# One schedule table of a fused RWKV-7 and squared-ReLU kernel exchanged for another

## Chip, cores and metric

The kernel runs on one core of one Trainium2 chip. The metric is the device time of one execution in microseconds (us). TensorE is called PE here, VectorE DVE, ScalarE ACT, GpSimd POOL, and the queue that issues most DMAs is SyncE's, SP.

## What is computed

For each of 4 batches and 8 heads a 40x40 state is carried over 768 steps, and the outputs go through a two-layer network with a squared ReLU:

```python
for t in range(S):                       # B=4, H=8, S=768, D=40
    y[:, :, t] = einsum('bhd,bhde->bhe', rt, state)
    Sa = einsum('bhde,bhe->bhd', state, at)
    state = state * wt[:, :, None, :] - einsum('bhd,bhe->bhde', Sa, bt) \
            + einsum('bhd,bhe->bhde', vt, kt)
x = y as (B*S, H*D)                      # 3072 x 320
h = x @ w_in                             # 320 -> 2048
out = maximum(h, 0)**2 @ w_out           # 2048 -> 320
```

## The kernel before

The 768 steps are cut into 6 chunks of 128. A chunk of one batch is a *piece* m (24 of them, m = 4 * chunk + batch); half a piece, four heads, is a *half* st (48). Four pieces of a chunk feed 8 *units* n of the network's first layer (48 units), and each piece has one output tile.

The life of a piece, by the names of the functions: six loads (`lW lK lB lA lV lR`, 160 KB each; R of pieces 0 to 15 comes for two chunks in one load of 320 KB); the decays (`b_ln` on ACT, `b_cs` on PE, `b_cx` on DVE, `b_xi` and `b_gp` on ACT); the products with the decays, rounded to bfloat16 (`b_pk` writes KBp, `b_pa`, `b_cv` and `b_cr` write their parts of RVAp, `b_gw` writes Gp); turned copies of them, by PE and a copy out of PSUM (`b_kt` and `b_kv` for KBT; `b_ta`/`b_at`, `b_vm`/`b_vv`, `b_rn`/`b_rv` for RV) or by a transposing DMA (`b_rt`, `b_aa`, `b_ka`, on SP's queue). Then for each half `st_a_mm` makes products `ca`, which are copied to CN with a triangular mask; `b_p`, `corr`, `b_c1`, `b_sn` solve for the piece's correction in the PSUM tile P; `b_x` sums its parts on POOL; `st_ex_mm` makes `ex`, copied to EX with the mask; `st_z`, `st_kb` make outputs and the next state in `uy`; `st_y`, `st_u` (DVE) move them to YN and UZ; `b_xt`, `b_xv` turn the outputs to XS. The network: `f_r`, `f_m` fill two PSUM tiles `hp`, `f_e` writes their ReLU to hs on ACT, `f_q` squares hs into Gt, `f_o` multiplies by WOUT, `f_v` copies `op_` to osb, `f_w` sends it out.

The order of all of it is written out by hand in one table, `ORDER`: 1937 tokens of the form `name.number`, with the PSUM bank behind `@` and the engine (D, A or P) behind `:` where there is a choice. Each engine takes its own tokens in that order and waits by semaphores; so do SP's loads.

```python
WORK = {"a": st_a_mm, "av0": bind(st_a_ev, 0), ..., "pk": b_pk, "pa": b_pa, ...}
def masked(by, out, in_):
    if by == "A":                        # plain copy on ACT, then a cut on POOL (cut_off)
        nc.scalar.activation(out=out, in_=in_[:], func=ACTF.Copy)
    else:                                # copy and mask in one, on DVE
        nc.vector.tensor_tensor(out=out, in0=in_[:], op=ALU.mult, in1=MEX...)
for tok in ORDER.split():
    act(tok)
```

So a mask on ACT costs ACT one instruction (line 346) and POOL one (line 353, AFFINE_SELECT); a mask on DVE (line 348) costs DVE one. Tokens `w` are matmuls without a use, which fill PE's waits at the start. The natural loads have four buffers a kind, hs two. The last two outputs (22 and 23) are copied and sent behind a branch, which a check of the numbers decides.

Of the kernel before, what the change touches and what calls it, by code (L numbers as in the profile page):

```python
# [18 lines left out]
def kernel(  # L19
# [23 lines left out]
    NB, NHH, T, D = r.shape  # L43
# [622 lines left out]
    def get_flag():  # L666
# [4 lines left out]
        lW.0 lK.0 f.0:D f.13:D f.1:P w.13@1 ln.0 w.2@u f.3:D lW.1 f.14:P f.17:P f.20:D lV.0 f.5:D  # L671
        lB.0 f.12:P i.0 f.19:D f.4:P w.15@x f.2:D ln.1 i.1 cv.0:A lK.1 w.3@e f.6:P w.1@u lA.0
        cs.0@e f.9:P cs.1@1 f.11:D xi.1 w.0@s lB.1 vm.0@u cx.0 xi.0 pk.0:D lA.1 w.8@s lV.1 f.8:P
        w.14@0 lR.0 gp.0 kt.0@f pa.0:D ta.0@f i.2 cx.1 vv.0:A f.18:D w.11@0 pk.1:P lW.2 w.9@u
        kv.0:D at.0:A a.0@xe f.16:D a.1@f0 f.10:D gp.1 kt.1@u pa.1:P av0.0:A av1.1:D w.6@1 ta.1@0
        kv.1:A w.4@s av1.0:D at.1:D a.2@fe av0.2:A aq0.0 w.16@1 lW.3 aq1.1 cv.1:A gw.0:D gc.0@0
        cr.0:P gl.0 ln.2 av0.1:D aq0.1 av1.2:D a.3@xu aq0.2 aq1.0 av0.3:A lK.2 aq0.3 w.7@1 cs.2@f
        p.0@1 gw.1:P rn.0@0 av1.3:D ln.3 aq1.2 cx.2 f.15:P m.0:A vm.1@x lR.1 aq1.3 rn.4@f k1.0
        lA.2 vv.1:A lB.2 p.1@s f.7:D cs.3@e lV.3 gp.2 c.0 lW.5 cr.1:A lK.3 m.1:D xi.2 rv.4:D xi.3
        pa.2:P k2.0 k1.1 c.1 s.0:A rv.0:A cx.3 pk.2:D gw.2:P k2.1 t.0@1 ta.2@f w.12@e s.1:A t.1@u  # L680
        x.1 tv.0:A tv.1:D at.2:A rn.5@0 e.1@xs rn.1@f ev1.1:D gp.3 rv.1:D rv.5:A lA.3 lB.3 kt.2@e
        e.3@0u cv.3:P ln.5 kv.2:D e.0@sf lW.4 a.4@fe ev0.1:A jk.1 eq1.1 ev0.0:D a.5@s1 pa.3:P
        eq0.1 cs.5@x av0.4:D av1.5:D lR.2 ev1.3:A ev0.3:A ta.3@1 xi.5 av1.4:D w.10@u pk.3:P aq0.4
        av0.5:A cx.5 kt.3@f aq1.5 z.1@0 e.2@es ev1.0:D ln.4 at.3:A kv.3:D eq1.3 kb.1 aq0.5 a.6@x1
        gl.1 wt.0 eq1.0 lV.2 lR.3 lA.4 ev0.2:A cs.4@u u.1 z.0@f av0.6:D lK.4 cv.2:P wt.2 eq0.0
        kb.0 av1.6:A y.1 x.0 z.3@e aq1.4 p.2@1 gp.5 cr.2:P en.1 lB.4 cx.4 eq0.3 m.2:D xi.4 u.0 y.0
        gp.4 a.7@xf k1.2 wt.6 vm.2@u aq1.6 lK.5 vm.3@0 c.2 av0.7:D pa.4:D aq0.6 wt.7 k2.2 cr.3:A
        eq0.2 av1.7:D lB.5 vv.2:D xt.0@x wd.0 rn.6@f lA.5 kb.3 s.2:A aq1.7 gw.3:P rn.2@1 gw.4:D
        ev1.2:A wd.1 ta.4@s lV.4 aq0.7 xv.0:A rn.7@u wt.3 wt.1 t.2@f p.3@x rv.6:D at.4:D rv.2:A
        m.3:D rv.7:A tv.2:A vv.3:D jk.2 wt.4 k1.3 rn.3@u e.4@ff lW.6 e.5@s0 y.3 eq1.2 c.3 pk.4:D  # L690
        k2.3 wt.5 ev0.4:A z.2@1 gl.2 s.3:D kt.4@f jk.0 kb.2 ev1.5:D u.3 kv.4:A eq0.4 u.2 x.2 t.3@e
        rv.3:A y.2 ev0.5:D gw.5:D xt.1@f ev1.4:D xv.1:A jk.3 a.8@ux a.9@ff tv.3:D eq1.4 fa.0 eq0.5
        e.6@e1 av0.8:A av1.9:A lK.6 pk.5:D fr.0@s0 wt.8 lV.5 ev0.6:D z.4@u ev1.6:D wt.9 kb.4 u.4
        z.6@f av0.9:A z.5@f lA.6 aq0.8 fb.0 pa.5:P eq1.6 eq1.5 ra.0 av1.8:A kb.5 aq0.9 y.4 gl.3
# [272 lines left out]
```

## Time and profile before

| | before |
|---|---|
| time, median of 3 runs | 258.82 us (258.47 to 259.81) |
| the profiled execution | 259.36 us, span 257.7 us |
| busy: PE, DVE, ACT, POOL | 243.3, 207.9, 207.8, 203.2 us |
| moved by DMA | 37.40 MB, 145 GB/s on average |

A busy PE is one with a matmul in flight; since matmuls overlap, that is no measure of how well it is fed, and idle time of PE is what is to be read. Lines such as L348 are lines of the kernel's file.

### The profile page before, as it was taken

The page shows a single profiled execution, that of the slowest core. Times are in us where ns is not written, and L with a number is a line of the kernel's source. Part 1 is how long each engine was busy: PE and PEld are TensorE (multiplying, and loading weights), DVE is VectorE, ACT ScalarE, POOL GpSimd, SP SyncE. Part 2 cuts the span into 40 slices and gives each one's busy share as a digit, 9 for nine tenths or more (in the row PEclk, how much of TensorE's full clock was granted, in tenths as well). Part 3 has the DMA queues.
Part 4 walks back from the last instruction along what each step waited for, and adds up shares of the span by engine and source line. Part 5 has one row for each costly group of instructions (what it writes and reads, how often), then busy time and mean ns, then how long its engine had stood idle before and what let it go on. Part 6 is the DMA issues. An engine that isn't in the chain of part 4 may idle for free.

```text
span 257.7 us, 9653 instructions
## 1 busy us (share of the span) xinstructions
PE 243.3 (94%) x3925; PEld 195.3 (76%) x3925; DVE 207.9 (81%) x435; ACT 207.8 (81%) x482; POOL 203.2 (79%) x235
## 2 busy tenths in 40 slices
PE   7986978999998999999999999999999999999992
PEld 3555666889886788787878888887888878888871
DVE  5597998799989899896999779989887799776220
ACT  3679898799987789887896799988796969799530
POOL 6469999839795499889789879888959777989770
PEclk9999997999999999999999999999999999999999
DMA  7999999999905997996999988988799985510011
GB/s 127 200 164 205 175 176 195 156 188 162 211 18 119 163 178 152 188 172 111 182 164 176 194 151 159 169 163 152 115 194 178 134 161 99 135 53 25 29 57 59
DMA packets 171924, 37.40 MB, mean 145 GB/s; under 512 B 167520, under 2 KB 170592, under 8 KB 171872
## 3 DMA queue, kind: packets, MB, share of 16 engines
q1 hardware_dynamic: 170528, 34.09, 76.1%
q0 software_dynamic: 1344, 2.62, 6.1%
q8 instruction: 32, 0.52, 0.9%
q14 instruction: 20, 0.16, 0.2%
HBM read 28.84 MB, written 3.93 MB: 127 GB/s over the span
## 4 chain that ended last, share of the span: by engine, by line
PE 64%; DVE 8%; DMA 8%; ACT 6%; SPq 5%; POOL 3%; issue 3%; POOLq 0%; DVEq 0%; ACTq 0%
PE hp L588 18%; SPq L95 4%; PE ex L456 4%; PE ca L333 3%; PE cs L191 3%; PE P L390 3%; PE uy L502 2%; PE tt L242 2%; DMA NRV<-in_r_dram 2%; DMA RV<-RVAp 2%; DMA NW<-in_w_dram 2%; DMA out_dram<-osb 2%; PE uy L497 2%; PE tb L434 1%; DVE EX L348 1%
## 5 line engine op out<-in xcount | busy, mean ns | idle before, releaser
L588 PE MATMUL hp<-XS,WIN 128*128 128x256 bf16 (+3 forms) x720 | 72.4, 255 | 0.0
L608 ACT ACTIVATE hs<-hp 128x512 bf16<-128x512 f32 x96 | 54.7, 601 | 11.6 <-PE hp L588 8.7
L588 PEld LDWEIGHTS <-WIN 128*128 128x128 bf16 (+1 forms) x720 | 49.2, 115 | 6.4 <-issue 3.6
L614 POOL TENSOR_TENSOR Gt<-hs 128x1024 bf16<-128x1024 bf16 x25 | 47.9, 1916 | 7.7 <-ACT hs L608 7.5
L623 PEld LDWEIGHTS <-Gt 128*128 128x128 bf16 x384 | 35.2, 97 | 12.0 <-issue 0.2
L348 DVE TENSOR_TENSOR EX<-ex,MEX 128x512 bf16<-128x512 f32 x61 | 40.2, 681 | 4.1 <-PE ex L456 4.0
L348 DVE TENSOR_TENSOR CN<-ca,MEX 128x512 bf16<-128x512 f32 x61 | 39.6, 681 | 4.5 <-PE ca L333 3.3
L353 POOL TENSOR_SCALAR_AFFINE_SELECT CN<-CN 128x512 bf16<-128x512 bf16 x35 | 22.8, 663 | 14.9 <-ACT CN L346 12.9
L353 POOL TENSOR_SCALAR_AFFINE_SELECT EX<-EX 128x512 bf16<-128x512 bf16 x35 | 23.5, 678 | 4.7 <-ACT EX L346 4.0
L614 DVE TENSOR_TENSOR Gt<-hs 128x1024 bf16<-128x1024 bf16 x23 | 21.3, 927 | 6.1 <-ACT hs L608 6.0
L220 POOL TENSOR_TENSOR KBp<-NKB,GI 128x640 bf16<-128x640 f32 x13 | 20.8, 1603 | 6.7 <-DMA NKB<-in_b_dram 5.2
L346 ACT ACTIVATE CN<-ca 128x512 bf16<-128x512 f32 x35 | 20.2, 599 | 7.3 <-PE ca L333 7.0
L411 ACT ACTIVATE jk<-CN 128x1024 bf16<-128x1024 bf16 x24 | 25.5, 1064 | 0.0
L346 ACT ACTIVATE EX<-ex 128x512 bf16<-128x512 f32 x35 | 20.5, 610 | 3.1 <-PE ex L456 2.8
L502 PE MATMUL uy<-KBp,EX 128*128 128x40 bf16 x384 | 21.9, 182 | 0.0
L407 POOL TENSOR_TENSOR Cc<-x,SN 128x320 bf16<-128x320 f32 x24 | 20.4, 848 | 1.9
L406 POOL TENSOR_TENSOR x<-Mc,c 128x320 f32<-128x320 bf16 x24 | 20.9, 870 | 0.3
L225 POOL TENSOR_TENSOR RVAp<-NA,GP 128x320 bf16<-128x320 f32 x16 | 14.4, 902 | 7.4 <-ACT GP L207 5.5
L333 PE MATMUL ca<-RV,KBT 64*128 64x128 bf16 x384 | 17.9, 217 | 1.9 <-DVE EX L348 1.2
L502 PEld LDWEIGHTS <-EX 128*128 128x128 bf16 x384 | 18.5, 98 | 1.0 <-issue 0.7
L390 PEld LDWEIGHTS <-CN 128*128 128x128 bf16 x384 | 15.0, 96 | 5.2 <-issue 3.4
L191 PE MATMUL cs<-lnW,UTI 128*128 128x320 f32 x48 | 18.4, 465 | 0.3 <-ACT lnW L186 0.3
(154 smaller groups left out, 632.1 us busy)
## 6 DMA issues: line engine op xcount, KB each, us to landing
NW<-in_w_dram SPq DMA_DIRECT2D x24, 160.0 KB, 3.8
NKB<-in_k_dram SPq DMA_DIRECT2D x24, 160.0 KB, 3.9
NRV<-in_v_dram SPq DMA_DIRECT2D x24, 160.0 KB, 4.0
NKB<-in_b_dram SPq DMA_DIRECT2D x24, 160.0 KB, 4.1
NA<-in_a_dram SPq DMA_DIRECT2D x24, 160.0 KB, 4.0
out_dram<-osb SPq DMA_DIRECT2D x24, 160.0 KB, 2.8
NRV<-in_r_dram SPq DMA_DIRECT2D x8, 320.0 KB, 4.5
WOUT<-in_moe_w_out_dram POOLq DMA_DIRECT2D x2, 640.0 KB, 7.9
```

Of the source, the lines that this page charges most:

```text
L191: nc.tensor.matmul(out=cs[:].rearrange("p h e -> p (h e)"), lhsT=UTI[:], rhs=bt[m].lnW[:], start=True, stop=True)
L333: nc.tensor.matmul(out=ca[s][:, i, u, :], lhsT=o.KBT[half(s), u, j0 + i, :], rhs=o.RVT[half(s), 2, j0 + i, :], start=(i == 0 and u == 0), ...
L346: nc.scalar.activation(out=out, in_=in_[:], func=ACTF.Copy)
L348: nc.vector.tensor_tensor(out=out, in0=in_[:], op=ALU.mult, in1=MEX[:].rearrange("p (i u) x -> p i u x", u=2))
L353: nc.gpsimd.affine_select(out=t_, in_=t_, pattern=[[0, 2], [0, 2], [1, L]], compare_op=ALU.is_gt, fill=0.0, base=0, channel_multiplier=-1)
L390: nc.tensor.matmul(out=Ps[m][:, h // 2, h % 2, 0:D], lhsT=CNs[m, "b"][:, h // 4, h // 2 % 2, h % 2, 1, :], rhs=X[:, h], start=False, stop= ...
L411: nc.scalar.activation(out=jk[:], in_=CNs[m, "b"][:].rearrange("p x i s u t -> p (x i s) u t")[:, :, 1, :], func=ACTF.Square, accum_out=AC ...
L502: nc.tensor.matmul(out=uy[:, (2 * i + s) * D:(2 * i + s + 1) * D], lhsT=EXs[st][:, i, s, u, :], rhs=o.KB[:, u, 2 * (j0 + i) + s, 0:D], sta ...
L588: nc.tensor.matmul(out=o.hp[u][:, i], lhsT=inner(g, rows, j), rhs=XSs[o.c][rows, g, o.bs, :], start=(o.begun[u] == 1), stop=(o.begun[u] > ...
L608: nc.scalar.activation(out=o.hs[:, u], func=ACTF.Relu, in_=o.hp[u][:].rearrange("p j a b -> p (j a b)"))
L614: engine("q", n).tensor_tensor(out=o.Gt[:, o.j0:o.j0 + 2 * o.per].rearrange("p j a b -> p (j a b)"), in0=hs, in1=hs, op=ALU.mult)
L623: nc.tensor.matmul(out=ops[n][:], rhs=WOUT[:, j, :], lhsT=Gts[h][:, b_, j, :] if h in SPLIT else Gts[h][:, j, b_, :], start=(j == 0), stop ...
```

## The change

Only the string `ORDER` differs: the same 1937 tokens in another order, 48 halves and 24 pieces as before, with other letters behind `:` and other banks behind `@`. No function and no shape differs. The first and the last two lines of it:

```diff
-        lW.0 lK.0 f.0:D f.13:D f.1:P w.13@1 ln.0 w.2@u f.3:D lW.1 f.14:P f.17:P f.20:D lV.0 f.5:D
+        lW.0 f.1:P lW.1 f.2:D ln.0 w.15@e f.0:P ln.1 i.0 lK.0 w.3@s lB.0 f.5:D lA.0 w.12@u f.16:D
...
-        ov.21:A es.0 o2.20 rb.47 o1.23@f o1.22@0 ow.21 ov.20:D o2.22 q.47:P gw.22:P o2.23 w.5@1
-        fl.0 w.17@s ow.20 w.18@1
+        o1.22@1 rb.47 ow.21 ow.19 q.45:D ov.20:D o2.22 o1.23@0 q.47:P o2.23 w.5@e w.17@s fl.0
+        w.18@e ow.20
```

Whole-program counts of what has another engine: of 192 masks 122 were on DVE and 70 on ACT (with 70 cuts on POOL), now 129 and 63. `b_pk` on DVE 11 and POOL 13, now 9 and 15; `b_pa` 8 and 16, now 5 and 19; `b_gw` 6 and 18, now 4 and 20; `f_q` 23 and 25, now 24 and 24.

What stands ahead of the first matmul of `b_p(6)` in the table, where the numbers of instructions differ:

| engine | before, after |
|---|---|
| DVE | RV copies from bf16 (`b_at`, `b_vv`) 4, 7; masks CN 18, 19 and EX 12, 11 (`av`, `ev`); `b_cx` 9, 8; `b_gw` 3, 1; `b_kv` 5, 4; `b_pa` 3, 2; fills 12, 11 |
| ACT | RV copies from bf16 10, 7; masks CN one fewer, EX one more; `b_cr` 2, 1; `b_kv` 2, 3; `b_jk` 5, 4; `st_energy` 2, 1 |
| POOL | cuts of CN one fewer; `b_cr` 2, 3; `b_gw` 4, 5; `b_pa` 5, 6; fills 9, 10 |

Ahead of `b_pa(8)` POOL has: one cut fewer, `b_cr` 2, 3; `b_gw` 5, 7; `b_pa` 5, 6; `b_pk` 3, 4 (the new one is `b_pk(8)`, which was on DVE); fills 9, 10.

Three places are shown as the built programs have them. First POOL's queue from the square of a unit to the products of piece 8 (x and Cc are `b_x`, RVAp<-NA,GP is `b_pa`, KBp<-NKB,GI `b_pk`). Before:

```order
L614 TENSOR_TENSOR Gt<-hs 128x1024
L216 TENSOR_TENSOR Gp_88<-NW,GP 32x8x40
L353 AFFINE_SELECT EX<-EX 128x2x256 x2
L406 TENSOR_TENSOR x_1969<-Mc,c_1241 128x320
L407 TENSOR_TENSOR Cc<-x_1969,SN_96 128x320
L168 CAST RVAp<-NRV 128x8x40
L406 TENSOR_TENSOR x_2003<-Mc,c_1397 128x320
L407 TENSOR_TENSOR Cc<-x_2003,SN_97 128x320
L225 TENSOR_TENSOR RVAp<-NA,GP 128x8x40
L220 TENSOR_TENSOR KBp_84<-NKB,GI 128x16x40
```

The row before the last is `b_pa(8)`, the last `b_pk(9)`. After:

```order
L216 TENSOR_TENSOR Gp_89<-NW,GP 32x8x40
L353 AFFINE_SELECT EX<-EX 128x2x256
L406 TENSOR_TENSOR x_1907<-Mc,c_1709 128x320
L407 TENSOR_TENSOR Cc<-x_1907,SN_95 128x320
L220 TENSOR_TENSOR KBp_83<-NKB,GI 128x16x40
L225 TENSOR_TENSOR RVAp<-NA,GP 128x8x40
L220 TENSOR_TENSOR KBp_84<-NKB,GI 128x16x40
L406 TENSOR_TENSOR x_2169<-Mc,c_1398 128x320
L407 TENSOR_TENSOR Cc<-x_2169,SN_97 128x320
```

`b_pk(8)` (KBp_83) has come to POOL and stands just ahead of `b_pa(8)`; one `b_x` went behind it.

Second, DVE at the same place. Before:

```order
L614 TENSOR_TENSOR Gt<-hs 128x1024
L518 TENSOR_TENSOR YN_100<-uy,GP 128x224
L225 TENSOR_TENSOR RVAp<-NA,GP 128x8x40
L614 TENSOR_TENSOR Gt<-hs 128x1024
L220 TENSOR_TENSOR KBp_83<-NKB,GI 128x16x40
L170 COPY osb<-op__1811 128x320
L170 COPY KBT<-tt 128x1024
```

After:

```order
L614 TENSOR_TENSOR Gt<-hs 128x1024
L170 COPY KBT<-tt 128x1024
L170 COPY TB<-tb 128x1024
L225 TENSOR_TENSOR RVAp<-NA,GP 128x8x40
L348 TENSOR_TENSOR EX<-ex_2098,MEX 128x2x256
L348 TENSOR_TENSOR EX<-ex_2099,MEX 128x2x256
L348 TENSOR_TENSOR CN<-ca_2121,MEX 128x2x256
L348 TENSOR_TENSOR CN<-ca_2122,MEX 128x2x256
L348 TENSOR_TENSOR CN<-ca_2136,MEX 128x2x256
L170 CAST RVAp<-NRV 128x2x8x40
L348 TENSOR_TENSOR EX<-ex_2203,MEX 128x2x256
L170 CAST RVAp<-NRV 128x2x8x40
```

DVE no longer makes KBp_83, and both casts of R for pieces 8 and 9 (`b_cr(9)`, then `b_cr(8)`, which was on POOL) are DVE's.

Third, SP's queue from the load of V of piece 9 on; RV_91<-RVAp is `b_rt(8)`, which needs `b_pa(8)`, and the two loads of R behind it are those of pieces 9 and 8. Before:

```order
L95 DMA NRV<-in_v_dram 128x8x40
L271 DMA_TRANSPOSE RV_91<-RVAp 128x8x128
L90 DMA NRV<-in_r_dram 128x8x80 x2
L95 DMA NW<-in_w_dram 128x8x40
L271 DMA_TRANSPOSE RV_92<-RVAp 128x8x128
L95 DMA NKB<-in_k_dram 128x8x40 x2
L95 DMA NRV<-in_v_dram 128x8x40
```

After:

```order
L95 DMA NRV<-in_v_dram 128x8x40
L271 DMA_TRANSPOSE RV_91<-RVAp 128x8x128
L90 DMA NRV<-in_r_dram 128x8x80 x2
L95 DMA NW<-in_w_dram 128x8x40
L634 DMA out_dram<-osb 128x320
L271 DMA_TRANSPOSE RV_92<-RVAp 128x8x128
L95 DMA NRV<-in_v_dram 128x8x40
L95 DMA NA<-in_a_dram 128x8x40
L95 DMA NKB<-in_k_dram 128x8x40
```

The loads of R stay behind that transpose; an output and two other loads have come ahead of the K of piece 10.

More of the change, by code (lines that the diff above doesn't have):

```diff
@@ L814 @@
[L814 to L817 removed]
+        lW.0 f.1:P lW.1 f.2:D ln.0 w.15@e f.0:P ln.1 i.0 lK.0 w.3@s lB.0 f.5:D lA.0 w.12@u f.16:D
+        lK.1 w.13@f f.3:P lV.0 f.20:D f.13:D f.10:P f.19:D f.8:D lB.1 w.1@0 f.12:P f.14:D cs.0@f
@@ new lines @@
+        xi.13 lA.13 fr.16@us e.21@10 s.11:A y.20 ra.16 gw.12:P ev1.21:D lW.15 t.11@e lV.13 fb.16
+        ev0.21:A tv.11:D a.25@xu rb.16 ow.2 a.24@10 e.22@fe av0.24:A pk.13:P eq0.21 av0.25:D
+        z.22@f av1.25:D aq0.24 ev0.22:A cs.14@s aq1.25 eq0.22 ev1.22:A z.21@x av1.24:D gp.13
+        eq1.21 kb.21 u.21 kt.13@1 gl.11 y.21 aq0.25 eq1.22 aq1.24 p.12@u fr.17@e0 cx.14 q.16:P
+        lA.14 m.12:A e.23@xf ev1.23:D lK.14 kb.22 lA.15 kv.13:A xi.14 k1.12 ev0.23:D gp.14 fa.17
+        pa.13:P eq1.23 z.23@1 c.12 fb.17 ln.16 cv.13:A eq0.23 xt.10@s kb.23 q.15:D lB.14 rt.13
```

281 lines of the change are left out of this document (137 added, 144 removed).

## Prediction

> **What bounds the kernel now.** I read the page first, then the busy time of each engine by stages, then the waits of the queues, then the stretch from 77 to 87 us instruction by instruction. The page's head gives the span and the load of each engine:
>
> ```profile
> span 257.7 us, 9653 instructions
> PE 243.3 (94%) x3925; PEld 195.3 (76%) x3925; DVE 207.9 (81%) x435; ACT 207.8 (81%) x482; POOL 203.2 (79%) x235
> ```
>
> Averages hide that the program has two halves with different limits. The table by stages (start:end, length, then busy time and instructions of PE, weight loads, DVE, ACT, POOL, the granted clock, the share of the DMA engines, GB/s) shows them:
>
> ```profile
> 18.00:30.00 12.00, 9.13 (x155) 6.64 (x154) 10.43 (x20) 10.68 (x28) 10.34 (x15) 1.00 1.04 182
> 30.00:42.20 12.20, 8.93 (x187) 7.53 (x183) 11.99 (x29) 11.92 (x27) 11.87 (x19) 1.00 1.04 174
> 42.20:45.60 3.40, 3.40 (x54) 3.01 (x53) 2.41 (x5) 2.28 (x5) 3.34 (x5) 0.50 1.26 204
> 45.60:50.00 4.40, 4.40 (x105) 3.99 (x102) 3.56 (x9) 2.73 (x7) 4.38 (x6) 1.00 0.83 142
> 50.00:55.00 5.00, 5.00 (x99) 4.17 (x96) 4.85 (x10) 5.00 (x13) 0.45 (x2) 1.00 1.04 179
> 55.00:64.00 9.00, 9.00 (x198) 8.03 (x193) 8.77 (x22) 8.81 (x22) 8.39 (x9) 1.00 1.07 172
> 64.00:70.00 6.00, 5.80 (x129) 5.21 (x127) 5.62 (x15) 5.86 (x15) 4.07 (x6) 1.00 1.14 212
> 70.00:80.00 10.00, 10.00 (x164) 8.05 (x162) 8.54 (x17) 8.41 (x22) 9.69 (x11) 1.00 0.16 31
> 80.00:85.00 5.00, 3.74 (x54) 2.69 (x53) 4.45 (x6) 2.71 (x5) 0.79 (x1) 1.00 1.05 213
> 85.00:95.00 10.00, 9.72 (x180) 8.31 (x175) 9.04 (x19) 9.08 (x20) 7.37 (x10) 1.00 1.11 161
> 95.00:251.00 156.00, 155.83 (x2491) 127.99 (x2491) 126.01 (x264) 128.71 (x301) 132.13 (x135) 1.00 0.78 138
> ```
>
> From 95 us on PE idles 0.17 us in 156: there PE is the limit, its instructions are the same in both programs, and work that the change moves between the other engines is hidden under PE. It cannot win there; it can only lose. From 30 to 42.2 us DVE, ACT and POOL are each busy over 97% while PE idles 3.27 us; from 18 to 30 PE idles 2.87 us. So between 18 and 42 us three vector engines are the limit together, and 6.1 us of PE are open. From 42.2 to 45.6 the clock was granted at 0.50: PE works all the time and does 1.7 us of work in 3.4. From 80 to 85 PE idles 1.26 us once more. Before 18 us the loads and the preparation set the pace, and both orders do `b_cs`, `b_kt`, `b_ta` and the first half's products in nearly the same succession; I take nothing there.
>
> **Term 1, the vector-bound stage.** What stands ahead of `b_p(6)`, which PE starts at about 64 us, is given with the change. The rows that price it, of the groups by shape (busy us, mean ns):
>
> ```profile
> L170 DVE COPY RV<-tt 128x512 bf16<-128x512 bf16 x5 | 2.1, 415 | 0.1
> L202 DVE TENSOR_TENSOR cx<-cs,lnW 128x320 f32<-128x320 f32 x24 | 11.6, 482 | 2.7 <-PE cs L191 1.8 <-ACT GI L197 0.8
> L216 DVE TENSOR_TENSOR Gp<-NW,GP 32x320 bf16<-32x320 f32 x6 | 3.8, 626 | 0.2
> L170 DVE COPY KBT<-tt 128x1024 bf16<-128x1024 bf16 x12 | 8.1, 677 | 0.4 <-PE tt L242 0.3
> L225 DVE TENSOR_TENSOR RVAp<-NA,GP 128x320 bf16<-128x320 f32 x8 | 5.2, 646 | 0.6 <-DMA NA<-in_a_dram 0.6
> L353 POOL TENSOR_SCALAR_AFFINE_SELECT CN<-CN 128x512 bf16<-128x512 bf16 x35 | 22.8, 663 | 14.9 <-ACT CN L346 12.9 <-DMA NW<-in_w_dram 1.8
> L168 POOL CAST RVAp<-NRV 128x640 bf16<-128x640 f32 x8 | 5.7, 717 | 1.1 <-issue 0.7 <-DMA NRV<-in_r_dram 0.4
> L216 POOL TENSOR_TENSOR Gp<-NW,GP 32x320 bf16<-32x320 f32 x18 | 16.0, 889 | 1.4
> L225 POOL TENSOR_TENSOR RVAp<-NA,GP 128x320 bf16<-128x320 f32 x16 | 14.4, 902 | 7.4 <-ACT GP L207 5.5 <-DMA NA<-in_a_dram 1.0 <-ACT SN L166 0.7
> L220 POOL TENSOR_TENSOR KBp<-NKB,GI 128x640 bf16<-128x640 f32 x13 | 20.8, 1603 | 6.7 <-DMA NKB<-in_b_dram 5.2 <-ACT GI L197 1.4
> L166 ACT ACTIVATE RV<-tt 128x512 bf16<-128x512 bf16 x11 | 6.7, 614 | 3.2 <-PE tt L242 3.2
> L411 ACT ACTIVATE jk<-CN 128x1024 bf16<-128x1024 bf16 x24 | 25.5, 1064 | 0.0
> ```
>
> DVE gets three more RV copies (3 x 0.415 = +1.25 us) and one mask more of CN and one fewer of EX (nothing); it loses one cx (-0.48), two Gp (-1.25), one KBT copy (-0.68) and one RVAp product (-0.65): -1.8 us in all. ACT loses three RV copies (-1.84) and one jk (-1.06); its other moves (a cast, a KBT copy, an energy sum) about cancel: some -2.9. POOL gets a cast (+0.72), a Gp (+0.89), an RVAp product (+0.90) and loses a cut (-0.66): +1.85. A fill that goes from DVE to POOL is at the very start and left out.
>
> Some of what DVE and ACT shed is only put off, past 64 us, where PE takes over; put off that far it is hidden. DVE is the engine whose results PE waits for most in this stage, so its 1.8 us bound the gain from above; if POOL, which was as full, becomes the one to wait for, its +1.85 is the other end. I take -1.5, nearer to DVE's row, because POOL, unlike DVE, has idle time right behind: 4.55 of 5 us from 50 to 55, and 7.1 us from 50 to 70.
>
> **Term 2, piece 8.** The 1.26 us of PE's idling between 80 and 85 have one cause:
>
> ```profile
> 79.30 2.03 DVE L614 TENSOR_TENSOR Gt<-hs 128x1024 bf16<-128x1024 bf16 x1
> 81.26 0.81 DVE L220 TENSOR_TENSOR KBp<-NKB,GI 128x640 bf16<-128x640 f32 x1
> ...
> L614 DVE TENSOR_TENSOR Gt<-hs x23: 673/745/2033, 52.2 to 243.3; 128x1024 bf16<-128x1024 bf16 x23
> ...
> 82.13 0.56 PE L242 MATMUL tt<-IDb,KBp 128*128 128x128 bf16 x7 [1.26 <-DVE KBp L220]
> ```
>
> DVE's square of a unit ran 2.03 us (the 23 squares on DVE, min/median/max: 673/745/2033 ns) beside POOL's product that began at 78.99; then came `b_pk(8)`, for which PE's `b_kt(8)` waited. In the new order `b_pk(8)` is POOL's, ahead of `b_pa(8)`, so this wait hangs on POOL:
>
> ```profile
> 77.71 1.32 POOL L225 TENSOR_TENSOR RVAp<-NA,GP 128x320 bf16<-128x320 f32 x1
> 78.99 1.80 POOL L220 TENSOR_TENSOR KBp<-NKB,GI 128x640 bf16<-128x640 f32 x1
> ```
>
> `b_pa(8)` ended at 79.03. Ahead of it POOL now has two Gp (+1.78), a cast (+0.72), an RVAp product (+0.90), `b_pk(8)` (+1.60), and one cut less (-0.66): +4.3 us, with a fill about +4.8. From 50 to 80 us POOL idled 7.4 us. If the new work fills 5.5 of these, `b_pa(8)` ends at 79.03 + 4.8 - 5.5 = 78.3 and `b_pk(8)` a microsecond before it, ahead of PE's need at 82.13 - 1.26 = 80.9 even if PE comes 1.5 us sooner, and the stall goes.
>
> What is late next is SP. Its queue stood for 12.2 us before `b_rt(8)`, until `b_pa(8)` was done; then it sent R of piece 9, which DVE cast at 86.50:
>
> ```profile
> SPq L271 <- POOL RVAp L225: 13.0, 2, 12.2
> 79.06 1.35 SPq L271 DMA_TRANSPOSE RV<-RVAp  x1
> 80.53 0.50 SPq L90 DMA_DIRECT2D NRV<-in_r_dram  x1
> 86.50 0.81 DVE L170 CAST RVAp<-NRV 128x640 bf16<-128x640 f32 x1
> NRV<-in_r_dram SPq DMA_DIRECT2D x8, 320.0 KB, 4.5
> ```
>
> So R of piece 9 is there 1.5 + 4.5 = 6.0 us after `b_pa(8)`: at 85.0 before, 1.5 us ahead of its use, and at 84.3 by the end assumed above. DVE then cannot gain more than 86.50 - 84.3 = 2.2 us at this point, whatever was won earlier. Term 1 has 1.5 of it; term 2 is the other -0.7. Its ends are -1.26 (the whole stall) and +3.3 (the third rival).
>
> The Trainium skill, page "SBUF — State Buffer", section "SBUF: two separate sides", says that a DVE instruction with two SBUF inputs and a GpSimd one that reads SBUF take turns under a lock, the second blocked for the whole of the first. The 2.03 us square agrees in kind. By that rule POOL's 1.6 us products, more of them now, can hold up any DVE square for as long, and the sum would be 257.6 instead of 256.6, an estimate from the two rows above (one stretch more of about a microsecond); the median square took 745 ns, so such stretches are the exception, and I stay with the sum.
>
> **The rest.** The clock's drop at 42.2 us follows twelve microseconds in which PE idled 3.27; the new order idles less there, but not by much, so I leave the 1.7 us as they are. Ends: -1.7 if there is no drop, +1.7 for a second. The Trainium skill ("TensorE: Matmul & The Clock Gate", section "Part 1: The HAM clock gate") puts the clock at half after an idle window of about 3.4 us, with a phase of its own; the length of 3.40 us at 0.50 here agrees, and the phase is why I do not bet on either end. From 95 us on: 0, with a loss possible where a result is now late. The 7 masks that go from ACT to DVE over the whole program, and POOL's 3 us or so more, are covered there: PE is busy 155.83 of 156 us, the others at most 85%. If that cover were gone, the worst comparable stage is 80 to 95, with 1.54 us of idle PE in 15. The tail (the last product, its copy and its send behind the branch) is the same: 0.
>
> **Sum.** The profiled execution took 259.36 us, 0.54 over the median of 258.82. 259.36 - 1.5 - 0.7 = 257.16; set against the median, 256.6 us.
>
> **Rivals.** First, *no change*: POOL takes DVE's place between 18 and 60 us. For it: POOL is as full as DVE there (11.87 of 12.20) and gets +1.85 where DVE sheds 1.8. Against it: the idling of POOL right after. The gain of term 1 is then lost, and with PE not earlier, term 2 brings little: 258.8 us.
>
> Second, *the clock*: a second stage at half speed, 258.82 + 1.7 = 260.5 us, or none at all and both terms at their best: 258.82 - 1.8 - 1.26 - 1.7 = 254.1 us.
>
> Third, *slower: POOL is late for piece 8 and SP stands behind it*. If POOL's idling from 50 to 70 us is not filled, because its next instruction again waits for ACT, `b_pa(8)` ends 4.8 us later, at 83.8. SP keeps R of pieces 9 and 8 behind `b_rt(8)`, and both casts are now DVE's, in order, with masks behind and between them: R lands at 83.8 + 6.0 = 89.8, DVE stands from 86.5 on, and PE waits for the masks behind it. Price 3.3 us: 258.82 + 3.3 = 262.1. It begins to decide where `b_pa(8)` ends after 86.5 - 6.0 = 80.5. For it: the 12.2 us row, and K and B of pieces 10 and 11, which now stand behind an output and two other loads. Against it: `b_pk` and `b_gw`, which POOL gets more of, need less than `b_pa` does, so POOL can start sooner on them.
>
> **Chances.** The forecast 0.48, with its own range 254.1 to 257.5; no change 0.22; slower, by the third rival (0.26) or a second clock drop (0.04), 0.30. About 0.5% (1.3 us) is what a measurement of this kernel can tell from no change, so faster means below 257.5 and slower above 260.1. The range runs from the best ends of the terms to the third rival: 254.1 to 262.1.
>
> **What would show it.** Right: between 18 and 42 us PE idles under 5 us; POOL's idling from 50 to 70 falls to about 2 us; `b_pa(8)` ends before 80 us; no wait over 0.5 us of PE for KBp near 81; from 95 us on nothing differs. Wrong: DVE idle before its cast of R near 86 us, a wait of SP over 12 us before the transpose, a second stage at 0.50, or PE idle after 95 us.

## The result, and the profile after

The new kernel takes 256.5 us (median of 6 runs, 255.77 to 256.94) against 259.59 us for the old one (median of 6, 258.47 to 260.67): a ratio of 0.9879, 95% interval 0.9847 to 0.9911. The forecast was 256.6 us. The total is right; its parts are not. The ratios here and below leave out executions over 1.5% above the fastest of their kernel, the longest of them one of after_weights (274.97 us, granted clock 0.843). The profiled execution took 255.77 us. Its head (the span, and each engine's busy time):

```profile
span 254.1 us, 9656 instructions
PE 240.7 (95%) x3925; PEld 194.5 (77%) x3925; DVE 203.2 (80%) x430; ACT 207.2 (82%) x478; POOL 206.4 (81%) x237
```

The table by stages of the new kernel, with the columns of the one in the prediction:

```profile
18.00:30.00 12.00, 9.78 (x162) 7.05 (x163) 11.12 (x25) 9.58 (x25) 10.33 (x14) 1.00 0.99 176
30.00:42.20 12.20, 7.55 (x159) 6.10 (x159) 10.78 (x24) 10.59 (x23) 11.05 (x18) 1.00 1.00 172
42.20:45.60 3.40, 3.40 (x81) 3.02 (x77) 3.40 (x10) 2.93 (x6) 3.31 (x7) 1.00 1.01 174
45.60:50.00 4.40, 3.08 (x66) 2.55 (x65) 2.99 (x7) 3.05 (x7) 4.24 (x5) 1.00 0.74 129
50.00:55.00 5.00, 5.00 (x99) 4.39 (x97) 3.84 (x8) 4.34 (x12) 1.77 (x3) 1.00 0.97 167
55.00:64.00 9.00, 9.00 (x210) 8.22 (x208) 8.63 (x21) 8.33 (x23) 8.79 (x10) 1.00 0.97 158
64.00:70.00 6.00, 6.00 (x133) 5.38 (x133) 5.37 (x14) 5.77 (x16) 5.82 (x6) 1.00 1.03 175
80.00:85.00 5.00, 4.93 (x64) 3.59 (x59) 4.16 (x8) 3.77 (x9) 4.92 (x5) 1.00 0.82 177
95.00:248.00 153.00, 153.00 (x2469) 126.47 (x2468) 121.30 (x256) 130.56 (x300) 127.04 (x129) 1.00 0.83 142
```

Two things are to be seen. Between 30 and 42.2 us DVE, ACT and POOL all have more idle time than before (1.42, 1.61 and 1.15 us, where they had 0.21 to 0.33), and PE nevertheless idles 4.65 us, where it idled 3.27. And the clock stays at 1.00 from 42.2 to 45.6, where the old profile has 0.50.

Where the time went is best read from when PE begins a piece's `b_p`. These are the matmuls of pieces 6, 9 and 23 (start, length, engine), first in the old profile:

```profile
64.29 0.36 PE L377 MATMUL P<-RVAp,CN 128*128 128x40 bf16 x8
95.71 0.36 PE L377 MATMUL P<-RVAp,CN 128*128 128x40 bf16 x8
225.51 0.36 PE L377 MATMUL P<-RVAp,CN 128*128 128x40 bf16 x8
```

and then in the new one:

```profile
64.67 0.36 PE L377 MATMUL P<-RVAp,CN 128*128 128x40 bf16 x8
94.09 0.36 PE L377 MATMUL P<-RVAp,CN 128*128 128x40 bf16 x8
222.66 0.36 PE L377 MATMUL P<-RVAp,CN 128*128 128x40 bf16 x8
```

Up to `b_p(6)` the new order is 0.4 us later, although its clock never dropped. From `b_p(6)` to `b_p(9)` it takes 29.42 instead of 31.42 us (-2.0), from `b_p(9)` to `b_p(23)` 128.57 instead of 129.80 (-1.2). The other 0.7 of the 3.6 us between the spans (257.7 - 254.1) fall behind, nearly all of it after the start of the last matmul.

PE's waits in the new profile (engine, line, what it waited for, total, times, longest) begin with one that the prediction did not have, for the network's first weights. SP's stand before `b_rt(8)`, which was one wait of 12.2 us for POOL's `b_pa(8)`, is now two in a row: 6.6 us (the longest of the three in the second row) until ACT's cast of V into RVAp is done, then 2.7 for POOL. So SP still stands there for 9.3 us:

```profile
PE hp L588 <- DMA WIN<-in_moe_w_in_dram: 1.3, 2, 1.0
SPq L271 <- ACT RVAp L166: 8.2, 3, 6.6
SPq L271 <- POOL RVAp L225: 2.7, 1, 2.7
```

Piece 8 in the new timeline (start, length, engine):

```profile
76.83 1.55 POOL L220 TENSOR_TENSOR KBp<-NKB,GI 128x640 bf16<-128x640 f32 x1
78.33 0.68 DVE L614 TENSOR_TENSOR Gt<-hs 128x1024 bf16<-128x1024 bf16 x1
78.33 1.39 POOL L225 TENSOR_TENSOR RVAp<-NA,GP 128x320 bf16<-128x320 f32 x1
79.75 1.35 SPq L271 DMA_TRANSPOSE RV<-RVAp  x1
81.21 1.20 SPq L90 DMA_DIRECT2D NRV<-in_r_dram  x2
85.87 0.49 DVE L170 CAST RVAp<-NRV 128x640 bf16<-128x640 f32 x1 [0.27 <-DMA NRV<-in_r_dram]
```

`b_pk(8)` and `b_pa(8)` stand on POOL as planned, `b_pa(8)` ends at 79.72 (before: 79.03), the transpose follows at once, and DVE waits 0.27 us for R of piece 9 (one of the prediction's signs of being wrong, though a short one). PE's stall of 1.26 us for KBp is gone.

### The profile page after: what moved, and what is told of

Same layout as the page of the kernel before. It is cut to its first block, busy times and chain, and to the rows that moved or that the text cites. A ratio compares the mean times of both kernels' runs of the same rounds, so it can differ in the third digit from the quotient of the medians.

```text
span 254.1 us, 9656 instructions
## 1 busy us (share of the span) xinstructions
PE 240.7 (95%) x3925; PEld 194.5 (77%) x3925; DVE 203.2 (80%) x430; ACT 207.2 (82%) x478; POOL 206.4 (81%) x237
## 4 chain that ended last, share of the span: by engine, by line
PE 69%; POOL 8%; ACT 7%; DMA 6%; SPq 5%; issue 1%; DVE 1%; POOLq 0%; DVEq 0%; ACTq 0%
PE hp L588 19%; SPq L95 4%; PE ca L333 4%; PE cs L191 4%; PE ex L456 4%; PE P L390 3%; DMA WIN<-in_moe_w_in_dram 3%; PE uy L502 3%; PE tt L242 3%; DMA NKB<-in_b_dram 2%; PE uy L497 2%; PE tb L434 2%; ACT EX L346 2%; POOL Gt L614 1%; POOL EX L353 1%
## 5 line engine op out<-in xcount | busy, mean ns | idle before, releaser
L588 PE MATMUL hp<-XS,WIN 128*128 128x256 bf16 (+3 forms) x720 | 71.2, 253 | 1.3 <-DMA WIN<-in_moe_w_in_dram 1.3
L588 PEld LDWEIGHTS <-WIN 128*128 128x128 bf16 (+1 forms) x720 | 48.8, 114 | 8.5 <-issue 4.2
L614 POOL TENSOR_TENSOR Gt<-hs 128x1024 bf16<-128x1024 bf16 x24 | 45.4, 1895 | 9.5 <-ACT hs L608 9.2
L348 DVE TENSOR_TENSOR CN<-ca,MEX 128x512 bf16<-128x512 f32 x66 | 42.7, 683 | 5.1 <-PE ca L333 4.5
L220 POOL TENSOR_TENSOR KBp<-NKB,GI 128x640 bf16<-128x640 f32 x15 | 23.7, 1579 | 4.0 <-ACT GI L197 3.7
L353 POOL TENSOR_SCALAR_AFFINE_SELECT CN<-CN 128x512 bf16<-128x512 bf16 x30 | 20.0, 675 | 5.9 <-ACT CN L346 5.6
L346 ACT ACTIVATE CN<-ca 128x512 bf16<-128x512 f32 x30 | 17.4, 596 | 6.6 <-PE ca L333 6.5
L225 POOL TENSOR_TENSOR RVAp<-NA,GP 128x320 bf16<-128x320 f32 x19 | 18.0, 946 | 5.8 <-ACT GP L207 4.3
L614 DVE TENSOR_TENSOR Gt<-hs 128x1024 bf16<-128x1024 bf16 x24 | 18.7, 783 | 3.5 <-ACT hs L608 3.5
L346 ACT ACTIVATE EX<-ex 128x512 bf16<-128x512 f32 x33 | 18.9, 597 | 2.9 <-PE ex L456 1.8
L216 POOL TENSOR_TENSOR Gp<-NW,GP 32x320 bf16<-32x320 f32 x20 | 17.5, 879 | 3.6 <-ACT GP L207 1.5
L333 PE MATMUL ca<-RV,KBT 64*128 64x128 bf16 x384 | 17.6, 217 | 1.0 <-ACT KBT L166 0.7
```

Of the source, the lines that this page charges most:

```text
L220: engine("pk", m).tensor_tensor(out=bt[m].KB[:, 0:2, :, 0:D], in0=nat.pop(("KB", m))[:], op=ALU.mult, in1=bt[m].GI[:].rearrange("p (u h) e ...
L333: nc.tensor.matmul(out=ca[s][:, i, u, :], lhsT=o.KBT[half(s), u, j0 + i, :], rhs=o.RVT[half(s), 2, j0 + i, :], start=(i == 0 and u == 0), ...
L353: nc.gpsimd.affine_select(out=t_, in_=t_, pattern=[[0, 2], [0, 2], [1, L]], compare_op=ALU.is_gt, fill=0.0, base=0, channel_multiplier=-1)
L588: nc.tensor.matmul(out=o.hp[u][:, i], lhsT=inner(g, rows, j), rhs=XSs[o.c][rows, g, o.bs, :], start=(o.begun[u] == 1), stop=(o.begun[u] > ...
L614: engine("q", n).tensor_tensor(out=o.Gt[:, o.j0:o.j0 + 2 * o.per].rearrange("p j a b -> p (j a b)"), in0=hs, in1=hs, op=ALU.mult)
```

## The experiments

An order cut from two tables nearly keeps the pace of its parts: from `b_p(9)` to `b_p(23)` the eight profiles with the new table there take 128.56 to 128.77 us, three with the old one 129.51 to 130.05. So the profile of each kernel tells more than its median. The table gives, from each kernel's profiled execution, the start of `b_p(4)`, how long the clock stood at 0.50 before it, and the time from `b_p(6)` to `b_p(9)` and from there to `b_p(23)`, worked out from starts like those above. Ratios are to the old kernel in the same set of runs.

| kernel | `b_p(4)` | at 0.50 | (6) to (9) | (9) to (23) | ratio, 95% interval |
|---|---|---|---|---|---|
| before | 49.74 | 3.4 | 31.42 | 129.80 | 1 |
| after | 50.43 | 0 | 29.42 | 128.57 | 0.9879 (0.9847 to 0.9911) |
| after_to_65 | 50.41 | 6.8 | 32.37 | 129.51 | 1.0019 (0.9981 to 1.0058) |
| before_to_72 | 48.76 | 0 | 31.46 | 128.56 | 0.9915 (0.9875 to 0.9955) |
| after_to_95 | 51.72 | 13.7 | 29.31 | 130.05 | 0.9940 (0.9908 to 0.9973) |
| before_to_95 | 50.53 | 3.4 | 31.43 | 128.77 | 0.9897 (0.9850 to 0.9945) |
| before_to_55 | 50.48 | 3.4 | 30.18 | 128.56 | 0.9890 (0.9832 to 0.9947) |
| before_pk8_pool | 49.02 | 0 | 30.99 | 132.42 | 1.0066 (1.0028 to 1.0104) |
| after_pk8_dve | 50.54 | 6.8 | 31.46 | 128.57 | 14,876 us, by another branch |
| back_order | 48.85 | 0 | 31.43 | 141.72 | 273.14 us, one run |
| back_engines | 49.13 | 0 | 31.43 | 145.84 | 279.55 us, one run |
| after_weights | 49.48 | 3.4 | 29.76 | 128.56 | 0.9889 (0.9830 to 0.9949) |
| after_again | 48.86 | 0 | 29.31 | 128.62 | 0.9888 (0.9831 to 0.9945) |
| after_weights_warm | 49.24 | 0 | 29.49 | 128.57 | 0.9833 (0.9786 to 0.9880) |

**Which part of the table brings the gain.** Four kernels take the first part of one table and the rest of the other; five to seven tokens change sides at a seam. The edits, each as the string around its seam (`||`), the last tokens of the first table and the first of the second:

```diff
+ after_to_65:  (new) ... s.6:A y.11 a.15@u0 q.4:P u.11 a.14@fe || u.45 en.7 lV.8 lB.8 ln.9 cv.7:A wo.1 ... (old)
+ before_to_72: (old) ... lK.9 ev1.13:D fr.7@e0 fa.7 cs.9@f aq1.15 || u.43 u.44 q.5:P rb.6 z.12@e ra.7 lB.9 ... (new)
+ after_to_95:  (new) ... aq0.19 xv.6:A lK.11 ev1.17:D cx.11 aq0.18 || lB.11 lA.12 pk.10:D eq0.16 x.7 pa.10:P p.9@f ... (old)
+ before_to_95: (old) ... aq1.18 xt.7@e ev1.17:D aq0.19 pa.10:P cx.11 || u.47 ow.1 rb.11 xv.6:A p.9@f ... (new)
```

> Kernel: the new table up to b_t(6) (about 66 us), then the old table's tokens in the old order. Theory (from the two traces): the first 65 us are no faster, b_p(6) starts at 64.7 us instead of 64.3, and the whole gain of 3.1 us lies behind; so 259.6 + 0.4 = 260.0 us, within 1 us. Rival, the forecast's term 1: the gain of the vector-bound stage is real and the profiled run of the new kernel only hides it: 259.6 - 1.5 = 258.1 us, and b_p(6) at about 63 us.

Measured 1.0019 (0.9981 to 1.0058): no gain, as the theory had it. The forecast's term 1 would have been 0.9942, outside the interval. But the ratio alone doesn't exclude a small gain, since from `b_p(6)` to `b_p(9)`, behind the seam, this kernel takes 0.95 us more than the old one. What speaks against term 1 is that `b_p(6)` came at 64.66 us (after 6.8 us at half speed).

> Kernel: the old table up to b_p(7)'s neighbour st_z(12) (about 72 us), then the new table's. Theory: nearly all of the gain of 3.1 us is behind this point: 259.6 - 3.1 = 256.5 us, or down to 256.0 since b_p(6) keeps its 0.4 us lead. The wait of PE of 1.26 us for KBp of piece 8 is gone. Rival, the forecast's split: only piece 8's 0.7 us lies here, 258.9 us.

Measured 0.9915 (0.9875 to 0.9955), between the theory's 0.988 and the rival's 0.9973, and only the theory's is inside. The profile says why it falls short: from `b_p(6)` to `b_p(9)` this kernel takes 31.46 us, as the old one does, though the wait for KBp is gone; waits of 0.56 and 0.28 us at 67 and 72 us, around the seam, and one of 0.50 us for a transposing DMA at 84 have come instead.

> Kernel: the new table up to b_p(9) (about 94 us), then the old one's. Theory: b_p(9) starts 1.6 us sooner as in the new kernel, and the old order from there on loses the 1.2 us that came between b_p(9) and b_p(23) and the 0.8 us of the tail: 259.6 - 1.6 = 258.0 us. Rival (forecast): nothing happens behind 95 us, so all of the gain is here: 256.5 us.

Measured 0.9940 (0.9908 to 0.9973); the theory's 258.0 us is 0.9938, and the rival's 0.988 is outside.

> Kernel: the old table up to b_p(9) (about 96 us), then the new one's. Theory: 1.2 us of small gaps between matmuls and 0.8 us of the tail are won behind 95 us: 259.6 - 2.0 = 257.6 us. Rival (forecast): PE is the limit there with the same instructions, so nothing: 259.6 us, or more.

Measured 0.9897 (0.9850 to 0.9945): a gain where the forecast allowed none; the theory's 257.6 us is 0.9923. In the profiles of these two kernels `b_p(9)` and `b_p(23)` start, new part last and old part last in turn:

```profile
96.50 0.36 PE L377 MATMUL P<-RVAp,CN 128*128 128x40 bf16 x8
225.27 0.36 PE L377 MATMUL P<-RVAp,CN 128*128 128x40 bf16 x8
```

```profile
95.26 0.36 PE L377 MATMUL P<-RVAp,CN 128*128 128x40 bf16 x8
225.31 0.36 PE L377 MATMUL P<-RVAp,CN 128*128 128x40 bf16 x8
```

128.77 us with the new table behind 95 us, 130.05 with the old one: the 1.2 us belong to the order behind 95 us and not to what came before. The ratio of before_to_95 would be 2.7 us, twice that. The rest goes with the clock: its four executions at a granted clock of 0.996 or more have a median of 257.58 us, the old kernel's ten such executions in the same set one of 258.77, 1.2 us more.

**Old front, new rest.**

```diff
+ before_to_55: (old) ... ev0.8:A c.5 ev1.8:A pa.6:P ta.6@u vv.5:A || u.43 u.44 eq0.8 xt.3@0 ev0.9:A eq1.8 z.8@s ... (new)
```

> Kernel: the old table up to st_z(8) (about 55 us), then the new one's. Counting the gaps between starts of matmuls beyond their own pace, the two profiles give the new order 0.7 us more of them up to b_p(4), though the clock never dropped in it, and 0.3 + 2.0 + 1.3 us fewer behind. Theory: the new front is a loss of 0.7 to 1.7 us and the rest is a gain of about 3.6, so this table beats both: 259.6 - 3.6 = 256.0 us against 256.5 of the new one, and 254.5 us where the clock does not drop (new: 255.8). PE gaps from b_p(6) to b_p(9) 2.3 us as in the new kernel (4.3 in the old). Rival: the gain between 64 and 95 us hangs on the state the new front leaves behind; then the gaps there stay over 3.5 us and the time is 257.5 us or more.

Measured 0.9890 (0.9832 to 0.9947), which holds both sides (0.986 and 0.992) and is no better than the new table. The profile lies between them: from `b_p(6)` to `b_p(9)` it took 30.18 us, 0.8 more than the new table whole, so a part of the gain there does hang on what the front leaves behind. PE waits for a transposing DMA in its place (the row's bracket: idle time and what ended it):

```profile
84.58 0.62 PE L333 MATMUL ca<-RV,KBT 64*128 64x128 bf16 x16 [0.83 <-DMA RV<-RVAp]
```

**Piece 8 alone, in both directions.** First the old table with `b_pk(8)` moved, then the new one with it put back:

```diff
- k2.7 gl.7 x.5 pa.8:P rt.8 xv.5:D ... fr.8@fe fr.9@uf pk.9:P pk.8:D ra.8 fb.8
+ k2.7 gl.7 x.5 pk.8:P pa.8:P rt.8 xv.5:D ... fr.8@fe fr.9@uf pk.9:P ra.8 fb.8
```

```diff
- xt.5@f q.7:D kb.12 pk.8:P kb.13 ... y.13 en.3 q.6:D gp.9 kv.8:D
+ xt.5@f q.7:D kb.12 kb.13 ... y.13 en.3 q.6:D pk.8:D gp.9 kv.8:D
```

> Kernel: the old table with one token moved: b_pk(8) on POOL just ahead of b_pa(8), not on DVE. Theory (the forecast's term 2): PE's wait of 1.26 us for KBp near 82 us goes; but b_pa(8) ends 1.5 us later (80.6 us), so R of piece 9 lands at about 86.6 and DVE's cast of it waits; PE's gaps from b_p(6) to b_p(9) fall from 4.3 to between 3.0 and 4.0 us, the time by 0.3 to 1.3 us. Rival (the forecast's third): R is late by enough that the masks behind it stop PE; the gaps there reach 5 us or more and the time rises by 1 us or more.

Measured 1.0066 (1.0028 to 1.0104): slower by 1.7 us. From `b_p(6)` to `b_p(9)` it won 0.43 us, within the theory's bracket; but from `b_p(9)` to `b_p(23)` it lost 2.6, of which neither side spoke. Rows of its timeline:

```profile
78.98 1.11 POOL L225 TENSOR_TENSOR RVAp<-NA,GP 128x320 bf16<-128x320 f32 x1
83.50 0.62 PE L333 MATMUL ca<-RV,KBT 64*128 64x128 bf16 x16 [0.94 <-DMA RV<-RVAp]
110.49 0.44 ACT L166 ACTIVATE osb<-op__2724 128x320 f32<-128x320 f32 x1 [1.45 <-DMA out_dram<-osb]
110.97 0.87 PE L252 MATMUL tt<-IDb,RVAp 128*128 128x128 bf16 x8 [1.09 <-ACT osb L166]
131.84 0.47 ACT L186 ACTIVATE lnW<-NW 128x320 f32<-128x320 f32 x1 [1.79 <-DMA NW<-in_w_dram]
135.09 0.40 PE L333 MATMUL ca<-RV,KBT 64*128 64x128 bf16 x8 [0.80 <-ACT hs L608]
```

The stall for KBp becomes 0.94 us of waiting for the transpose behind `b_pa(8)`, which now ends at 80.09. Later two things that only SP's queue delivers come late, and the two waits of PE behind them make up 1.9 of the 2.6 us: the buffer of an output (ACT's copy waits 1.45 us for its DMA, and PE 1.09 us for ACT), and W of a later piece (ACT waits 1.79 us, and PE for ACT's ReLU behind it). The first is shown by the brackets; for the second that the ReLU is late because `lnW` was is read from ACT's order, not tried by itself. This is the forecast's third rival in kind, found in another kernel and further back than I had put it.

> Kernel: the new table with b_pk(8) put back on DVE, behind the square of unit 6 as in the old one. Theory: piece 8's move is needed in the new order: PE waits for KBp again, the gaps from b_p(6) to b_p(9) rise from 2.3 to 3.3 us or more, and the time by 0.7 to 1.3 us, to 257.5 us or so. Rival: POOL, 1.6 us less loaded, ends b_pa(8) sooner, R of piece 9 comes sooner, and that pays for the wait: gaps 2.3 us, no change.

The edit does more than put the step back. In this table `b_kt(8)`, with which PE turns KBp, stands five tokens ahead of `pk.8:D`; in the old one it stands ten behind. So PE reads KBp of piece 8 before DVE has written it, no wait for KBp can arise, and neither the theory nor the rival is put to the test. Wrong products are reason enough for the branch in front of the last outputs to have gone to the part that computes everything step by step, as it did in all four executions (14,876 us); that they are the reason was not tried by itself. The trace up to there shows only what DVE's 1.41 us more do to the order around them:

```profile
79.05 0.61 PE L242 MATMUL tt<-IDb,KBp 128*128 128x128 bf16 x8
79.77 1.41 DVE L220 TENSOR_TENSOR KBp<-NKB,GI 128x640 bf16<-128x640 f32 x1
85.66 0.40 PE L333 MATMUL ca<-RV,KBT 64*128 64x128 bf16 x8 [1.32 <-DVE EX L348]
```

PE waits 1.32 us for the masks that DVE makes behind the product, and from `b_p(6)` to `b_p(9)` it takes 31.46 us where the new table takes 29.42. From `b_p(9)` on it runs as the new table does (128.57 us). So the one move costs 1.7 us in the old order; what it is worth inside the new one is not shown.

**Order or engines, behind 95 us.** One kernel has the new order and banks there with the engines of the old table, the other the old order and banks with the engines of the new. Two of the 77 letters that differ:

```diff
  back_order, against before_to_95:
- xv.7:A ... q.10:P
+ xv.7:D ... q.10:D
  back_engines, against before:
- xv.7:D ... q.10:D
+ xv.7:A ... q.10:P
```

> Kernel: the old table up to b_p(9) (95 us); behind it the new order and the new banks, but every step on the engine of the old table (77 letters put back). From the start of b_p(9) to that of the last matmul the old kernel takes 157.0 us, the new one 155.7, the table that changes there 155.9. Theory: what removes the gaps there is the order (which step stands ahead of which on PE, and the banks), not the engines: 155.9 us, within 0.3. Rival: it is the engines (7 cuts of POOL fewer, masks done in one instruction on DVE): 157.0 us.

Measured 273.14 us: from `b_p(9)` to the last matmul it takes 171.6 us. Both the theory (155.9) and the rival (157.0) are refuted; neither the order with its banks nor the engines carry the gain alone. PE's waits in it are now headed by one for POOL's cuts, which the old order with its own engines did not have:

```profile
PE uy L502 <- POOL EX L353: 4.3, 2, 2.7
```

> Kernel: the old table and the old order and banks throughout, but behind b_p(9) every step on the engine that the new table gives it (77 letters). The mirror of the kernel with the new order on the old engines, which took 171.6 us from the start of b_p(9) to that of the last matmul where the old one takes 157.0 and the new one 155.7. Theory: an engine's letter fits only the order it was made with, so this is slower as well, 162 us or more for that stretch (265 us in all). Rival: the new letters are better whatever the order (7 cuts fewer), 156 us.

Measured 279.55 us, 177.5 us for that stretch: the same in the mirror, as its theory had it. In these two tables a step's engine and its place in the order are one choice.

**The front: weights and clock.** In the new table the last three loads of the network's first weights are moved up on POOL's queue; a second kernel adds seven tokens `w` at PE's longest stands (first of the lines below the weights, then the fillers), and the new table runs unchanged beside it.

```diff
- ... lV.4 wt.4 eq0.4 ev1.4:D ... u.43 wt.9 a.8@ux ... z.4@u wt.5 wt.8 lW.6 ...
+ ... lV.4 wt.4 wt.9 wt.5 wt.8 eq0.4 ev1.4:D ... u.43 a.8@ux ... z.4@u lW.6 ...
- ... kt.2@x ... rn.2@0 ... e.4@1e ... a.8@ux ... e.6@e1 ...
+ ... w.19@1 kt.2@x ... w.20@f w.21@f rn.2@0 ... w.22@f w.23@f e.4@1e ... w.24@f a.8@ux ... w.25@f e.6@e1 ...
```

> Kernel: the new table with the last three loads of the network's first weights (9, 5, 8) moved up on POOL's queue to right behind load 4, so that they are issued at about 37.4 to 39 us, not 39.6 to 42.8. Theory: PE's waits of 1.13 and 0.54 us for WIN at 48 us go, and 1 to 1.6 us come off b_p(4): 256.5 - 1.3 = 255.2 us. Rival: the three issues (0.53 us each) hold POOL's cuts and sums behind them, and the work of PE that waits for those takes the gain: 256.5 us, with the gaps up to b_p(4) unchanged at 17.2 us.

Measured 0.9889 (0.9830 to 0.9949), the new table's ratio. The wait for WIN is gone from PE's list and `b_p(4)` starts at 49.48 in spite of 3.4 us at half clock, but part came back as a wait before `b_p(9)` (29.76 us instead of 29.42), and the time shows no gain. The clock in the five executions behind the ratio was 0.972 to 0.991, so that a gain may be hidden under it.

> Kernel: the new table, unchanged, on the same chip and among the same runs as the next one, so that the two can be compared. Expected: ratio 0.988 to the old kernel as before; 256 to 257.5 us; in the runs whose clock stays at 1.0, 255.8 us.

Measured 0.9888 (0.9831 to 0.9945), profiled at 253.98 us. This same table starts `b_p(4)` at 48.86 here, 50.43 in its first profile, both times without a drop of the clock: the front alone varies by 1.6 us from one execution to the next. The wait for WIN is 0.5 us in this one and 1.3 in the other.

> Kernel: the new table with the three weight loads moved up, and with seven tokens w more (two matmuls without a use each, 0.43 us) put ahead of the steps where PE stood longest between 20 and 43 us: one ahead of b_kt(2), two ahead of b_rn(2), two ahead of st_ex_mm(4), one each ahead of st_a_mm(8) and st_ex_mm(6). Theory: the half-speed stages follow windows of 3.4 us in which PE is busy for less than about 0.62; with the fillers no window from 18 to 43 us falls below 0.65, the clock stays at 1.0 in nearly every run, and b_p(4) starts 1 us sooner than in the new kernel: 255.0 to 255.5 us, 1 us under the new one of the same runs. Rival: PE's time there is given by the vector engines, so a half-speed stage costs nothing and the fillers only delay what stands behind them; b_p(4) starts at 50.4 us or later and the time is that of the new table or longer by up to 1 us.

Measured 0.9833 (0.9786 to 0.9880): 255.24 us, median of six from 254.86 to 256.00. The clock is 0.996 or more in all six. The stages around the fillers, first without them (after_weights), then with them:

```profile
30.00:42.20 12.20, 8.46 (x147) 6.78 (x144) 9.92 (x23) 10.10 (x22) 11.20 (x18) 0.86 1.08 179
42.20:50.00 7.80, 7.41 (x174) 6.76 (x173) 7.25 (x18) 7.08 (x16) 7.19 (x8) 1.00 0.92 165
```

```profile
30.00:42.20 12.20, 9.83 (x149) 6.26 (x145) 9.58 (x24) 10.19 (x22) 11.51 (x18) 1.00 1.10 183
42.20:50.00 7.80, 7.80 (x178) 6.99 (x178) 7.21 (x18) 7.28 (x16) 7.28 (x8) 1.00 0.95 168
```

The fillers make PE busy 9.83 us instead of 8.46 and the clock is granted whole, and `b_p(4)` comes 0.24 us sooner for it, not a microsecond. Against the old kernel this is the best table that was run; against the new one its ratio is lower by 0.0055, with intervals that overlap, so that it is faster than the new table is likely and not shown. Two executions of the new table in the same set that kept a clock of 0.996 or more took 253.98 and 255.69 us, much as these six do. So it may be that the fillers change no more than how often the clock drops, and with it the spread: the new table's six run from 253.98 to 258.11 us.

## Why the prediction was right, and where it was not

**Term 1 (-1.5) failed: no run shows a gain of that size.** The step that failed is "I take -1.5, nearer to DVE's row": it took what DVE sheds, counted in busy time, for what PE gains. In the new profile all three engines have room between 30 and 42 us and PE waits longer, so that their load is not what sets the end there. PE's waits from 18 to 42.2 us show what took DVE's place, and it is not POOL, the rival that the prediction had, but ACT, which was to shed the most (-2.9). The longest, first before, then after:

```profile
PE P L390 <- DVE Mc L172: 1.4, 2, 1.0
PE ca L333 <- DVE EX L348: 1.2, 2, 0.7
```

```profile
PE tt L252 <- ACT CN L346: 0.9, 1, 0.9
PE ex L456 <- ACT RV L166: 0.8, 1, 0.8
PE ca L333 <- ACT KBT L166: 0.7, 1, 0.7
```

In sum, by what came last, PE waited there 5.0 us for DVE and 0.8 for ACT in the old profile, 3.0 and 3.9 in the new one; other executions without a clock drop agree (before_to_72: 5.0 and 1.1; after_again: 2.2 and 3.8). "PE idles under 5 us from 18 to 42" measured 6.87 (2.22 + 4.65). Four executions of the old front without a clock drop start `b_p(6)` at 63.31 to 63.68 us, two of the new one at 63.10 and 64.67: between 0.6 sooner and 1.4 later, with 1.3 us of the worse one waiting for WIN, which my list of moved instructions did not price.

**Term 2 (-0.7) named the right wait and was too small: -2.0.** `b_pa(8)` before 80 us (79.72), no wait for KBp, as said; POOL's idling from 50 to 70 us fell from 7.1 to 3.6, not to 2. The limit by R was set right too: DVE's cast came 0.63 us sooner, at 85.87, and had to wait 0.27. But the term was capped at what DVE could gain at that cast, and PE gained at other places as well: PE's gaps (the start of the next matmul less the start of this one and its line's usual spacing, such as 109 ns for a 128x256 of L588, summed) fall by 0.43 us from `b_p(6)` to `b_p(7)`, by 1.30 to `b_p(8)` and by 0.26 to `b_p(9)`. One thing gained is DVE's square, which ran 2.03 us at 79.30 in the old order: the one at 78.33 in the new order runs 0.68, and none of its 24 is over 1.11. So the longer sum that the prediction worked out for squares held up beside POOL's products did not come. And the gain was credited to removing one wait: with the one token moved, the old order lost 1.7 us. Which of the moved tokens bring the 2.0 us together stays open.

**From 95 us on (0, "it can only lose"): -1.3.** The step that failed is "PE is busy 155.83 of 156 us, so PE is the limit". A matmul's record is longer than its spacing to the next (a record of L333 lasts 217 ns on average), so that short stands lie under the record before. From the start of `b_p(9)` to that of the last matmul the same 2492 matmuls take 157.03 us in the old profile and 155.73 in the new one. Of these 1.30 us 0.9 are four stands of 0.22 to 0.24 us in the old order, beyond the usual spacing, where the new one has none over 0.15. One of them, with the weight load that shows it; no idle time of PE itself stands in the profile there:

```profile
111.25 0.21 PEld L252 LDWEIGHTS <-RVAp 128*128 128x128 bf16 x3 [0.20 <-issue]
```

**The tail (0) stands.** 0.7 us of the spans' difference lie behind the start of the last matmul (4.9 and 4.3 us), but the kernels above that end with the old table have 4.2 to 5.1 us there, those with the new one 4.1 to 4.9: that is no part of the change.

**The clock ("unchanged, -1.7 or +1.7").** The price was about right; whether it stays unchanged is open. One stage of 3.4 us at half speed takes the mean granted clock to 0.993, as in the old profile. Of the old kernel's 26 executions behind the ratios of after_to_65 to before_to_95, the ten at 0.996 or more have a median of 258.77 us, the others 260.57: 1.8 us. The old profile, from which the sum was made, had lost it. In that set one of 22 executions with the new front reached 0.996, and 20 of 44 with the old front; in the set of after_again it was two of four and three of nine. So the new front may drop more often, a cost that the prediction put at nothing. But the price does not grow with the length: without a drop the old front starts `b_p(4)` at 48.76 to 49.13 us, with one of 3.4 us at 49.74 to 50.53; the new front starts it at 48.86 and 50.43 without a drop, at 50.41 with 6.8 us at half speed and at 51.72 with 13.7. PE stands for part of such a stage in any case: in those 13.65 us it was busy for 11.38.

**The rivals.** "No change" had the right word for the front (ACT, more than POOL, took DVE's place), and the rest made up for it. "Slower by POOL late and SP behind it" did not happen here: `b_pa(8)` ended 0.8 us ahead of the point from which it was to decide. It is what happened when the one step was moved alone. That the total came out is luck. In the pair of profiles the errors are +1.9 us in term 1 against -1.3 in term 2, -1.3 behind 95 us and -0.7 in a tail that is not the change's: -3.6 us where the sum had -2.2. As a ratio the forecast was 256.6 / 258.82 = 0.9914, just outside the interval; the old kernel's median rose by 0.8 us with the later runs.

## What to carry to other kernels

Load taken from busy engines brought nothing in the front of this kernel: PE's waits went from one engine to the other. Name the wait that ends last, and compare the starts of the same instruction in both profiles, stage by stage, before believing a sum of durations. A stretch in which PE reads as busy all the time could still be made 0.8% shorter: read the spacing of its matmuls. In a hand-written order a move that removes a stall need not pay by itself: it cost 1.7 us in the old table, where an output buffer and a load on SP's queue then came late. And see that a moved step still stands ahead of those that read what it writes, or its time tells nothing of the move.

## What was not expected of the hardware

The clock fell to half for 3.41 us or a multiple (6.83, 13.65), each time right behind a stretch of 3.41 us in which PE was busy for 0.55 to 0.65 of the time. Such a pair in the profile of after_weights:

```profile
34.43:37.85 3.42, 1.91 (x43) 1.41 (x41) 2.28 (x6) 2.93 (x7) 3.41 (x8) 1.00 1.21 202
37.85:41.26 3.41, 3.23 (x44) 2.65 (x41) 2.89 (x7) 2.35 (x5) 3.33 (x5) 0.50 1.00 163
```

No single stand of PE in the stretches ahead of the drops lasts more than 1.1 us. The length agrees with the 3.4 us window of the Trainium skill ("TensorE: Matmul & The Clock Gate", section "Part 1: The HAM clock gate"), which speaks of an idle window; here the drops came behind windows that were more than half busy. It is not a sharp bound, such as the 0.62 that an expectation above puts down: the old profile's drop came behind 0.65, while in this kernel the stretch before that pair, at 0.57, passed without a drop, and in the new kernel's first profile two at 0.63 and 0.65 did. And a long half-speed stage cost far less than its length: 13.7 us of it at most 2.9 (51.72 against 48.86, the best start of `b_p(4)` with that front), where half the speed of a full PE would have cost 6.8, an estimate from its length.
